# Preparation products of a chunked delta-rule attention: which engine makes them

## The chip, the cores and the metric

The kernel runs on one core of a Trainium2 chip. The metric is device time of one launch in microseconds. Three runs of the kernel before gave 1052.31 us as their median (1048.45 to 1052.65).

## The reference, cut to what matters

Attention is a recurrence over 768 steps for 32 heads of 40 by 40 state; its output feeds a mixture of experts with two of eight experts per token.

```python
for t in range(S):                       # attention, per head
    y[:, :, t] = einsum('bhd,bhde->bhe', rt, state)
    Sa = einsum('bhde,bhe->bhd', state, at)
    state = state * wt[:, :, None, :] - einsum('bhd,bhe->bhde', Sa, bt) \
            + einsum('bhd,bhe->bhde', vt, kt)
# experts: noisy top-2 gate, then for each expert e
h = maximum(x[mask] @ w1[e], 0.0)
out[mask] += top2_w[mask, k, None] * (h @ w2[e])
```

## The kernel before, in words

The recurrence is computed in chunks of 64 steps. There are twelve chunk positions for each of two halves `p` of the batch, so the main loop (`run`) has 24 turns `n`; turn `n` belongs to group `n//4` (six groups of two chunk positions), chunk `c` and half `p`. A group is prepared before its turns come, by three functions.

- `prepA(g,p)` loads the decays `raww` and the operands `rawba` (b and a). VectorE scans the decays (`Gx`, L495). ScalarE takes logarithm and exponential (L498, L499), VectorE makes a refined reciprocal `NH` from it (L501 to L504). Then come the products that this case is about: `NG_` (called G here), L506, a product of `Gx` with a scale; b by `NH`, L518; a by `NG_`, L520. `pack` splits each of b and a into two fp16 halves: the first by ScalarE (L459), the second by VectorE (L460); the result goes to DRAM (`d_ab`), and comes back in another layout (`st_ab`). `scoresL` multiplies b with a on TensorE, ScalarE copies the scores out (`lt`, `lo`, L556), and they go to DRAM (`scr`).
- `tsolve(g)` loads the scores of both halves as `X` (L563), masks them (L564) and inverts the triangular blocks in 30 pairs of a product and a sum (L570, L571). For groups zero and one this runs on VectorE, for groups two to five on GpSimd. The result goes to DRAM and comes back as `T` (L593).
- `prepC(g,p)` loads `rawk`, multiplies it by `NH` in two halves (L544), packs it (L459, L460) and stores it.

A turn (`chain`, `outp`, `pre`, `blocks`) is a chain of TensorE bursts (L470), ScalarE copies (`w` L473, `q` L652, `vu` L657, `sE` L630) and VectorE operations: `sfs` L625, `vu` L658, the state `Sst` L667, `ak` L606, `P` L680 twice, `uT` L474, `xT` L99, `xt` L691. L101 is the matmul of the expert gate, which ScalarE's `xT` (L98) feeds.

Buffers: one `rawba`, one `rawk`, one `Gx`, two `pk`, six `NG_` (`NGB`, so G of a group reuses the buffer of the group three before, after its last turn's transposes `pgm`), five `st_ab`. The preparation of group `g` is written into the loop seven turns (`LA`) and four turns (`LC`) ahead. A planner with its own cost estimates orders the instructions of every engine; the chain has a priority of 1500. Each engine then runs its list in that order. Before, G is made by GpSimd in all groups, b and a by VectorE in groups zero and one and by GpSimd after that, k by VectorE in group zero and by GpSimd after that. After attention the experts run, from 620 us on, almost wholly on TensorE.

Of the kernel before, what the change touches and what calls it, by code (L numbers as in the profile page):

```python
# [403 lines left out]
class Att:  # L404
# [81 lines left out]
    def prepA(s,p,g):  # L486
# [30 lines left out]
        dv=d.rearrange("l p x n->p l x n")  # L517
        (V if g in MD else nc.gpsimd).tensor_tensor(b_,b_,fl(NH),op=ALU.mult)  # L518
        s.pack(b_,-SC,1,1,V=V,out=lambda pk: nc.sync.dma_start(dv[:,:,1],pk))
        (V if g in MD else nc.gpsimd).tensor_tensor(a_,a_,fl(NG_),op=ALU.mult)  # L520
        s.pack(a_,-SC,0,1,V=V,out=lambda pk: nc.sync.dma_start(dv[:,:,0],pk))
# [244 lines left out]

BAB=1; RKB=1
SAB=5
MD=(0,1); MG=(); MK=(0,); TG=0
GA=-1; GC=-1  # L770
def HB(k=0): return [(h,b^k) for h in range(8) for b in range(2)]

# [125 lines left out]
```

## Time and profile before

| | value |
|---|---|
| median of the runs | 1052.31 us |
| profiled execution | 1041.7 us, span 1039.9 us |
| mean granted TensorE clock | 0.913 |
| busy: PE, DVE, ACT, POOL | 819.7, 543.8, 389.8, 399.2 us |
| hardware DMA queue q1 | 41.4% of the 16 engines' span |

DVE is VectorE, ACT is ScalarE, POOL is GpSimd, PE is TensorE. Busy time is an average over stages: attention with its preparation fills the first 620 us, the experts the rest. A profiled execution is one launch; its time differs from the runs' median.

### The profile page before, as it was taken

What the parts mean: (1) busy time and instruction counts of PE and PEld (TensorE: products, weight loads), DVE (VectorE), ACT (ScalarE), POOL (GpSimd) and SP (SyncE); (2) the same over time, 40 slices, a digit from 0 to 9 for tenths busy, and PEclk for the clock granted to TensorE, in tenths of its full rate; (3) what the DMA queues carried; (4) which work ended last, traced back from release to release, by engine and by line L of the source; (5) the groups of instructions that cost most, each with busy time, mean ns of one, the idle gap of its engine ahead of it and who ended that gap; (6) DMA issues with size and microseconds to landing.
All of it is one profiled execution on the core that took longest, in us unless ns stands there. A gap on an engine that the chain in (4) does not pass through costs nothing.

```text
span 1039.9 us, 27444 instructions
## 1 busy us (share of the span) xinstructions
PE 819.7 (79%) x11706; PEld 716.3 (69%) x11706; DVE 543.8 (52%) x1150; ACT 389.8 (37%) x820; POOL 399.2 (38%) x504
## 2 busy tenths in 40 slices
PE   0113456769888758888988789999999999999994
PEld 0113345557666646777766668899899999999994
DVE  9268568554469774338554753633443434343420
ACT  2202333335445433444442432525243535343420
POOL 6102241167659778219301004335151516160312
PEclk9999998779869866988996789999999999999998
DMA  4793996387588484473494402435252525252303
GB/s 119 177 235 91 254 249 152 93 226 198 124 213 249 126 206 110 110 160 108 138 280 147 135 14 43 120 93 133 58 133 67 131 64 133 61 137 59 35 8 37
DMA packets 127111, 135.88 MB, mean 131 GB/s; under 512 B 59249, under 2 KB 106805, under 8 KB 126901
## 3 DMA queue, kind: packets, MB, share of 16 engines
q1 hardware_dynamic: 116292, 114.90, 41.4%
q0 software_dynamic: 10688, 19.14, 9.7%
q8 instruction: 94, 1.54, 0.6%
q14 instruction: 37, 0.30, 0.1%
HBM read 96.25 MB, written 41.03 MB: 132 GB/s over the span
## 4 chain that ended last, share of the span: by engine, by line
PE 50%; POOL 13%; DMA 13%; DVE 11%; issue 5%; ACT 3%; SPq 2%; POOLq 0%; ACTq 0%; DVEq 0%
PE ph L287 17%; PE po L309 17%; POOL X L571 4%; POOL Tt L570 4%; DMA d_ab<-pk 3%; DMA rawk<-in_fm_dram 3%; PE psc L470 3%; PE pY L470 2%; PE pt L268 2%; PE pQ L470 2%; DVE X L571 1%; DVE Tt L570 1%; PE pW L470 1%; DMA d_k<-pk 1%; DMA X<-scr 1%
## 5 line engine op out<-in xcount | busy, mean ns | idle before, releaser
L311 POOL DMA_INDIRECT out_dram<-y,oi x56 | 92.2, 1647 | 233.7 <-ACT y L310 212.2
L290 DVE SCALAR_TENSOR_TENSOR hl<-ph,hh 128x256 fp32r<-128x256 f32 (+1 forms) x128 | 70.1, 555 | 120.4 <-ACT hh L288 113.2
L288 ACT ACTIVATE hh<-ph 128x320 fp32r<-128x320 f32 (+1 forms) x128 | 64.6, 518 | 147.7 <-PE ph L287 140.4
L470 PE MATMUL pQ<-w,T 32*32 32x40 f32 x2304 | 49.5, 229 | 48.4 <-ACT w L473 23.7
L470 PEld LDWEIGHTS pQ<-w,T 32*32 32x32 f32 x2304 | 42.2, 133 | 61.8 <-ACT w L473 26.3
L309 PE MATMUL po<-w2h,hh 128*128 128x320 f32 x384 | 74.8, 314 | 2.5 <-DVE y L304 1.9
L470 PE MATMUL psc<-RV,uT 128*64 128x128 f32 x384 | 65.3, 325 | 12.6 <-DVE P L680 12.1
L571 POOL TENSOR_TENSOR X<-X,Tt 128x30 f32<-128x30 f32 (+14 forms) x120 | 72.0, 600 | 8.2
L252 POOL DMA_INDIRECT xr<-xd,gi x56 | 53.7, 958 | 51.2 <-DVE oi L178 17.8
L309 PE MATMUL po<-w2h,hl 128*128 128x320 f32 x384 | 70.8, 311 | 0.0
L287 PE MATMUL ph<-xh,w1h 128*128 128x512 f32 (+1 forms) x256 | 69.7, 355 | 1.1 <-DVE hl L290 1.1
L570 POOL TENSOR_TENSOR Tt<-X 128x30 f32<-128x30 f32 (+14 forms) x120 | 67.2, 560 | 7.8
L287 PE MATMUL ph<-xh,w1l 128*128 128x512 f32 (+1 forms) x256 | 68.9, 350 | 0.0
L287 PE MATMUL ph<-xl,w1h 128*128 128x512 f32 (+1 forms) x256 | 68.6, 349 | 0.0
L470 PEld LDWEIGHTS psc<-RV,uT 128*64 128x64 f32 x384 | 51.7, 164 | 22.9 <-DVE P L680 13.0
L309 PE MATMUL po<-w2l,hh 128*128 128x320 f32 x384 | 65.7, 309 | 0.0
L309 PEld LDWEIGHTS po<-w2h,hh 128*128 128x128 f32 x384 | 61.0, 188 | 6.7 <-issue 2.3
L470 PE MATMUL psc<-RV 128*64 128x128 f32 x384 | 65.3, 325 | 0.0
L680 DVE TENSOR_TENSOR P<-psc,mk 128x512 f32<-128x512 f32 x48 | 32.9, 686 | 59.1 <-PE psc L470 59.1
L309 PEld LDWEIGHTS po<-w2h,hl 128*128 128x128 f32 x384 | 59.8, 188 | 0.5
L470 PEld LDWEIGHTS <-st_ab 120*64 120x64 f16 (+1 forms) x928 | 28.3, 123 | 44.1 <-issue 30.5
L309 PEld LDWEIGHTS po<-w2l,hh 128*128 128x128 f32 x384 | 58.6, 188 | 0.1
(314 smaller groups left out, 1936.2 us busy)
## 6 DMA issues: line engine op xcount, KB each, us to landing
w2r<-in_w_dram SPq DMA_DIRECT2D x8, 1280.0 KB
RV<-in_rv_dram SPq DMA_DIRECT2D x48, 192.0 KB
rawba<-in_fm_dram SPq DMA_DIRECT2D x24, 360.0 KB
d_ab<-pk SPq DMA_DIRECT2D x24, 360.0 KB
st_ab<-d_ab SPq DMA_DIRECT2D x36, 240.0 KB
w1r<-in_w_dram SPq DMA_DIRECT2D x8, 1024.0 KB
raww<-in_fm_dram SPq DMA_DIRECT2D x12, 365.6 KB
st_ab<-d_ab SPq DMA_DIRECT2D x24, 180.0 KB
```

What stands on the lines that cost most here:

```text
L252: k=t//128; nc.gpsimd.indirect_dma_start(out=X[:p,k if s.cap==CAP else 0],out_offset=None,in_=s.xd[int(w is not s.early[0])],in_offset=OFF ...
L268: for t,p in tiles(t0,n): nc.tensor.transpose(pt[:,t-t0:t-t0+p],x[:p,t//128,f0:f0+128],s.idm[:p,:p])
L287: for i,(a,b) in enumerate(mm): nc.tensor.matmul(ph[:,:n],a,b,start=i==0,stop=i==7)
L288: nc.scalar.activation(hh[:,f,:n],ph[:,:n],AF.Relu)
L290: if c.stop>c.start: nc.vector.scalar_tensor_tensor(o,ph[:,c],0.0,hh[:,f,c].bitcast(F32),op0=ALU.max,op1=ALU.subtract)
L309: s.lm=nc.tensor.matmul(po[:p],h[:,f,r],w[:,f],start=k==0,stop=k==23); k+=1
L311: st=nc.gpsimd.indirect_dma_start(out=s.out_d,out_offset=OFFS(ap=idx[:p,e,ii:ii+1],axis=0),in_=y[:p],in_offset=None,compute_op=ALU.add)
L470: def mm(s,*a,**k): return lambda: s.nc.tensor.matmul(*a,**k)
L570: eng.tensor_tensor(t,Xt[:,j:j+1,j+1:].to_broadcast([128,j,m]),Xt[:,0:j,j:j+1].to_broadcast([128,j,m]),op=ALU.mult)
L571: s.tl=eng.tensor_tensor(Xt[:,0:j,j+1:],Xt[:,0:j,j+1:],t,op=ALU.add)
L680: nc.vector.tensor_tensor(m,pp.rearrange("p i j t->p (i j) t"),s.mk.to_broadcast([128,8,64]),op=ALU.mult)
```

## The change

All three products go to VectorE in all groups. One other effect: the setup of the expert part's constants was ordered behind G of group zero (`after(pl)`); with 0 in `MG` it is not.

```diff
-MD=(0,1); MG=(); MK=(0,); TG=0
+MD=MG=MK=range(6); TG=0
```

The lines that read these names, unchanged (`V` is VectorE):

```python
s.pl=(V if g in MG else nc.gpsimd).tensor_tensor(NG_,Gx[:,:,0:64],nr[:,:,31:32]...,op=ALU.mult)  # L506
(V if g in MD else nc.gpsimd).tensor_tensor(b_,b_,fl(NH),op=ALU.mult)                             # L518
(V if g in MD else nc.gpsimd).tensor_tensor(a_,a_,fl(NG_),op=ALU.mult)                            # L520
(nc.vector if g in MK else nc.gpsimd).tensor_tensor(k1,k1,G['NH']...,op=ALU.mult)                 # L544, twice
with after(xd),(ExitStack() if 0 in MG else after(pl)): m.consts2(s.dm.bitcast(F32))              # run
```

## Rows read from the trace of the kernel before

**Rows 1.** Busy time by stretch: window, length, engines, granted clock, DMA share, GB/s.
```profile
85.00:160.00 75.00, 38.62 (x676) 32.11 (x678) 52.90 (x70) 28.29 (x54) 24.34 (x14) 1.00 0.84 218
160.00:410.00 250.00, 191.01 (x4405) 157.25 (x4403) 157.95 (x296) 103.00 (x238) 158.16 (x206) 0.80 0.66 170
```
**Rows 2.** Timeline of VectorE, state updates: start, length, engine, line, operation.
```profile
366.72 0.48 DVE L667 SCALAR_TENSOR_TENSOR Sst<-pS,gam 128x320 f32<-128x320 f32 x1
...
396.87 0.48 DVE L667 SCALAR_TENSOR_TENSOR Sst<-pS,gam 128x320 f32<-128x320 f32 x1
...
415.91 0.48 DVE L667 SCALAR_TENSOR_TENSOR Sst<-pS,gam 128x320 f32<-128x320 f32 x1
...
431.17 0.49 DVE L667 SCALAR_TENSOR_TENSOR Sst<-pS,gam 128x320 f32<-128x320 f32 x1 [1.63 <-PE pd L471]
```
**Rows 3.** Waits of ScalarE, 85 to 410 us: total, times, longest.
```profile
ACT pk L459 <- POOL rawba L518: 38.4, 8, 7.7
...
ACT pk L459 <- POOL rawba L520: 8.3, 6, 3.6
```
**Rows 4.** Timeline of ScalarE, packing; in brackets the idle time before and its end.
```profile
172.93 0.84 ACT L459 ACTIVATE pk<-rawba 120x768 f16<-120x768 f32 x1 [5.79 <-POOL rawba L518]
...
225.34 0.84 ACT L459 ACTIVATE pk<-rawba 120x768 f16<-120x768 f32 x1 [7.70 <-POOL rawba L518]
...
268.62 0.84 ACT L459 ACTIVATE pk<-rawba 120x768 f16<-120x768 f32 x1 [4.86 <-POOL rawba L518]
...
382.64 0.84 ACT L459 ACTIVATE pk<-rawba 120x768 f16<-120x768 f32 x1 [7.16 <-POOL rawba L518]
```
**Rows 5.** Timeline of TensorE: its idle time right behind those four.
```profile
174.15 1.27 PE L470 MATMUL pQ<-w,T 32*32 32x40 f32 x32 [6.31 <-ACT w L473]
...
228.49 0.25 PE L101 MATMUL pl<-wg,xT 128*128 128x16 f16 x3 [6.30 <-ACT xT L98]
...
269.92 0.76 PE L470 MATMUL pW<-q,lo 32*32 32x40 f32 x32 [1.76 <-ACT q L652]
...
384.77 1.28 PE L470 MATMUL pQ<-w,T 32*32 32x40 f32 x32 [6.72 <-ACT w L473]
```
**Rows 6.** Timeline of GpSimd: products of k ahead of the product of b.
```profile
168.89 2.09 POOL L544 TENSOR_TENSOR rawk<-rawk,NH 120x384 f32<-120x384 f32 x2 [18.81 <-DMA rawk<-in_fm_dram]
```
**Rows 7.** Timeline of VectorE, second half of the packing, with idle time before.
```profile
226.21 1.78 DVE L460 SCALAR_TENSOR_TENSOR pk<-rawba,pk 120x768 f16<-120x768 f32 x1 [7.47 <-ACT pk L459]
...
383.52 1.85 DVE L460 SCALAR_TENSOR_TENSOR pk<-rawba,pk 120x768 f16<-120x768 f32 x1 [7.46 <-ACT pk L459]
```
**Rows 8.** Groups by line: engine, count, busy us, mean ns, idle before.
```profile
L544 POOL TENSOR_TENSOR rawk<-rawk,NH 120x384 f32<-120x384 f32 x20 | 24.6, 1252 | 34.0 <-DMA rawk<-in_fm_dram 34.0
L518 POOL TENSOR_TENSOR rawba<-rawba,NH 120x768 f32<-120x768 f32 x8 | 14.6, 1825 | 6.5 <-DMA rawba<-in_fm_dram 6.5
...
L511 DVE TENSOR_TENSOR nge<-Gx,raww 120x12 f32<-120x12 f32 x10 | 6.4, 637 | 0.0
...
L544 DVE TENSOR_TENSOR rawk<-rawk,NH 120x384 f32<-120x384 f32 x4 | 2.0, 553 | 4.4 <-DMA rawk<-in_fm_dram 4.4
...
L514 DVE TENSOR_TENSOR gm<-nge,Gx 120x12 f32<-120x12 f32 x10 | 1.9, 191 | 0.0
L518 DVE TENSOR_TENSOR rawba<-rawba,NH 120x768 f32<-120x768 f32 x2 | 1.9, 952 | 1.0 <-DMA rawba<-in_fm_dram 1.0
```
**Rows 9.** Timelines of VectorE and GpSimd: a scan beside two steps of a solve.
```profile
333.16 2.08 DVE L495 TENSOR_TENSOR_SCAN Gx<-raww,d 120x780 f32<-120x780 f32 x1
...
332.94 0.66 POOL L570 TENSOR_TENSOR Tt<-X 128x234 f32<-128x234 f32 x1
333.68 2.00 POOL L571 TENSOR_TENSOR X<-X,Tt 128x234 f32<-128x234 f32 x1
```
**Rows 10.** Timeline of GpSimd: G products that waited, with what ended it.
```profile
279.48 1.48 POOL L506 TENSOR_TENSOR NG__4022<-Gx,raww 120x768 f32<-120x768 f32 x1 [6.07 <-PE pgm L471]
...
360.07 1.48 POOL L506 TENSOR_TENSOR NG__5505<-Gx,raww 120x768 f32<-120x768 f32 x1 [5.17 <-PE pgm L471]
```

## The prediction

> **What bounds the kernel now.** I read the busy times by stretch first. In the experts' stage, from 620 us on, TensorE is nearly always busy and nothing of the change runs there, so all of it must come from attention, and from the part where groups one to five are prepared, 85 to 410 us [rows 1]. There TensorE is busy 38.6 of 75 us and then 191.0 of 250 us, at a mean granted clock of 1.00 and 0.80; VectorE 52.9 + 158.0 = 210.9 of 325 us, 65%; GpSimd 182.5 us. No engine is full, so the turns are paced by waits. The next thing to read is the distance of two state updates: 30.2 us from 366.72 to 396.87, where group five is prepared, and 15.3 us from 415.91 to 431.17, where nothing is [rows 2]. A turn can thus go in half the time, and the preparation takes the rest.
>
> The view of waits says how. ScalarE waited 38.4 us, eight times, at L459 for the product of b (L518) from GpSimd, and 8.3 us, six times, for that of a (L520) [rows 3]. ScalarE runs its list in order: behind each packing stand the copies of the chain, and TensorE waits for those. The timelines show it: ScalarE idle 5.79, 7.70, 4.86 and 7.16 us [rows 4], and right behind each of the four TensorE idle 6.31, 6.30, 1.76 and 6.72 us, together 21.1 us, every time ended by a ScalarE copy [rows 5]. Why the product is late differs. Once the two products of k went first on GpSimd and themselves waited for their load [rows 6]; twice VectorE stood idle, 7.47 and 7.46 us, while GpSimd had the product to make [rows 7], and there part of the wait is that of the load of rawba, which the change leaves.
>
> **The change part by part.**
>
> *Products of b and a, groups two to five, 8 + 8.* One takes 1.825 us on GpSimd and 0.952 us on VectorE [rows 8]. The direct gain is 0.87 us each, and the product no longer stands behind solve steps and k products. What ScalarE's wait loses lies between 0.87 us and the whole wait. I take 4.4 of 6.31 us for the first of the four TensorE stalls (the k pair of 2.09 us and its load are out of the way), 2.1 of 6.30 for the second (the load is late, 0.87 plus a queue place), the whole 1.76 for the third, 2.6 of 6.72 for the fourth: 10.9 us. For the other waits of the 46.7 us, which are short or followed by little, 2 us. Sum -13 us; bounds 0 (the waits were all for loads) and -21 us (all four stalls go).
>
> *Products of k, groups one to five, 20 halves.* 1.252 us on GpSimd, 0.553 us on VectorE [rows 8]. They mostly wait for their load, 34.0 us of GpSimd's idle time, and are not late to ScalarE otherwise. Gain on the path: nothing; the wait that hides them is that for the load. If that cover went, 20 x 0.70 = 14 us would be to gain, which I leave out of the sum.
>
> *Products G, all groups, 12.* No row shows one on VectorE. I take 0.952 us, the row of L518, which has the same shape; the bounds are 0.553 us, the row of half that size, and 1.48 us, what GpSimd takes for it [rows 8, 10].
>
> *What VectorE gets.* 12 + 16 products at 0.952 us and 20 at 0.553 us: 26.7 + 11.1 = 37.7 us. It gets something back: the tiny L511 takes 637 ns where L514, of the same shape, takes 191 ns [rows 8]; L511 is issued right beside G. With G gone from GpSimd I take 10 x 0.45 = 4.5 us back. Net 33 us: VectorE's share of the 325 us goes from 65% to 75%. What of it lies on the path: a turn has nine VectorE operations that the chain waits for, and some 13 turns fall in the stretch, so 117 operations; each meets one of the new products with a chance of 33/325 = 0.10 and then waits for half of 0.95 us: 117 x 0.10 x 0.48 = 5.6 us. Bounds: 0 if the planner puts them into VectorE's idle 114 us, 33 us if all are in line with the chain. I take +5.6, near the lower bound, because VectorE stood idle at exactly the places where the products are needed [rows 7].
>
> *Solves of groups two to five.* They lose the products between their steps. Worth nothing by itself: no TensorE wait behind a solve's T shows among the four stalls, and a next solve waits for its X, not for GpSimd. What is late next is the load of rawba and the packing's DMA.
>
> *Setup of the expert constants, freed from its order.* GpSimd is idle then; nothing.
>
> The row of the scan shows that VectorE and GpSimd hinder each other: a solve step of 2.00 us beside a scan of 2.08 us, where the step before of the same shape took 0.66 us [rows 9]. The Trainium skill, "SBUF — State Buffer", section "Who interferes with whom", says that a VectorE instruction with two SBUF inputs and a GpSimd instruction that reads SBUF exclude each other for a whole instruction, whoever starts first; the trace agrees, with 2.00 against 0.66 us. This speaks against the change, since every moved product now runs beside the solves: by that rule each of the 30 products of groups three to five would wait half a step, 0.33 us, some 10 us on VectorE, of which the same sixth (5.6 of 33) reaches the chain: the sum would be 1.7 us worse, -5.7 us. I keep the sum without it, since the same rule gives back time where GpSimd's own products, twice as long, no longer hold VectorE.
>
> **Sum.** -13 + 5.6 = -7.4 us. The profiled execution took 1041.7 us, so 1034.3 us for one like it. That execution was 10.6 us below the median of the runs; the time is compared with runs, so 1052.3 - 7.4 = 1045 us.
>
> **The rivals.**
>
> *A. Products held on VectorE.* G reuses one of six buffers and may wait for a turn's transposes: 6.07 and 5.17 us on GpSimd, where only solves and products stood behind it [rows 10]. On VectorE the chain's P, vu and Sst stand behind it. If the planner places G too early by that wait in three of the six products of groups three to five, 3 x 5.6 = 17 us are added to every engine that waits for the chain: 1052.3 - 7.4 + 17 = 1062 us, slower. It decides from 7.4/5.6, two such places. For it: the planner's order is made from estimates. Against it: the scan that follows G on VectorE already waits for it and the order has kept that wait off the chain.
>
> *B. Loads, not products.* The ScalarE waits end with the load of rawba anyway, the gain is 0.87 us at each of the four stalls plus the 2 us for the rest, 5.5 us, and VectorE's 5.6 us take it back: 1052 us, no change. For it: VectorE's idle 7.46 us in front of the packing, in which the load was still on its way. Against it: two stalls of the four have another cause.
>
> *C. All stalls go, and the clock with them.* Four stalls 21.1 us, no cost on VectorE, and fewer idle gaps raise the granted clock of 0.80 in 160 to 410 us by 0.02 (each 0.01 is an estimated 2 us of TensorE's 191 us there): 21 + 4 = 25 us, 1027 us. For it: 15.3 us a turn is seen. Against it: VectorE's load is certain.
>
> *D. The planner reorders.* Another order of every engine for no reason of the products: some 10 us up, 1062 us.
>
> **How the numbers follow.** Forecast 0.45 (its own range 1035 to 1050), A 0.20, B 0.17, C 0.13, D 0.05. A difference below 0.5%, 5.3 us, can't be told from no change. Faster: C and 0.35 of the forecast's 0.45, 0.48. Same: B and the rest of the forecast, 0.27. Slower: A and D, 0.25. The range 1029 to 1063 us leaves out the ends of C and A.
>
> **What would show it right or wrong.** ScalarE's waits at L459 for a product should fall from 46.7 us to under 25 us, the waits for loads and packing's DMA stay; the four TensorE stalls should shrink to 10 us; VectorE's busy time should rise by 30 to 40 us and GpSimd's fall by some 72 us (24.6 + 14.6, the same 14.6 for a, and 12 x 1.48); the state updates of the turns around 366 us should come closer than 30.2 us. It is wrong if VectorE shows idle time in front of L506 ended by pgm, with P, vu or Sst behind it, or if the waits at L459 keep their length and only the engine's name in them changes.

## The result, and the profile after

The changed kernel takes 1036.85 us (median, 1035.52 to 1038.98), against 1051.84 us for the kernel before on the same chip: ratio 0.9883, 95% interval 0.9839 to 0.9926. It is faster: the medians differ by 15.0 us, the ratio is worth 12.3 us. The forecast was 1045 us with a range of 1029 to 1063. The time lies inside, but the gain is about twice the 7.4 us that were forecast, and it comes from elsewhere than the sum put it. The profiled execution took 1035.5 us, span 1033.7 us, mean granted clock 0.904.

The first view is the busy time by stretch of the kernel after, in the columns of [rows 1].

```profile
85.00:160.00 75.00, 43.14 (x801) 36.12 (x804) 54.98 (x89) 31.20 (x61) 0.00 (x0) 0.91 0.86 217
160.00:410.00 250.00, 185.97 (x4213) 154.04 (x4203) 165.32 (x319) 98.62 (x225) 110.76 (x177) 0.74 0.65 168
```

VectorE has 220.3 us of work in these 325 us, 68%, where [rows 1] have 210.9 us: 9.5 us more, though 46 of the 48 moved products fall into them, and the 48 add up to 42.1 us. GpSimd has nothing from 85 to 160 us. TensorE is idle 95.9 of the 325 us, where it was 95.4 before, and its granted clock is lower, 0.91 and 0.74 where it was 1.00 and 0.80. So in this part, from which the sum took its gain, TensorE has gained nothing.

The waits of ScalarE after, 85 to 410 us (total, times, longest), answer to [rows 3]:

```profile
ACT pk L459 <- DVE rawba L518: 22.7, 6, 7.2
...
ACT sfs L624 <- DVE Sst L667: 17.4, 8, 6.8
ACT pk L459 <- DVE rawba L520: 14.2, 5, 5.4
```

22.7 + 14.2 = 36.9 us, where the same two waits were 46.7 us. Mostly it is the engine's name that has changed. The same view for VectorE after (85 to 410 us) says why:

```profile
DVE rawk L544 <- DMA rawk<-in_fm_dram: 27.7, 8, 6.5
DVE P L680 <- PE psc L470: 16.8, 10, 5.1
DVE rawba L518 <- DMA rawba<-in_fm_dram: 14.5, 3, 5.5
```

The waits for the loads, 42.2 us, are now VectorE's own, and VectorE runs its list in order. Its timeline after shows what stands behind such a wait:

```profile
313.28 1.52 DVE L544 TENSOR_TENSOR rawk<-rawk,NH 120x384 f32<-120x384 f32 x2 [5.70 <-DMA rawk<-in_fm_dram]
314.72 0.55 DVE L99 SCALAR_TENSOR_TENSOR xT<-px,xT 128x384 f16<-128x384 f32 x1
315.19 0.47 DVE L667 SCALAR_TENSOR_TENSOR Sst<-pS,gam 128x320 f32<-128x320 f32 x1
```

The state update stands behind the product of k. ScalarE's next copy, in its own timeline, pays for it:

```profile
315.69 0.47 ACT L624 ACTIVATE sfs<-Sst 128x320 f16<-128x320 f32 x1 [6.00 <-DVE Sst L667]
```

TensorE's waits moved accordingly. Its view of waits, 85 to 410 us, first before, then after:

```profile
PE pQ L470 <- ACT w L473: 23.7, 9, 6.7
...
PE psc L470 <- DVE P L680: 9.9, 4, 5.1
```
```profile
PE psc L470 <- DVE P L680: 12.6, 4, 4.1
PE pY L470 <- DVE P L680: 9.1, 5, 4.1
PE pS L470 <- DVE vu L658: 8.2, 5, 4.1
PE pst L470 <- ACT sE L630: 6.8, 2, 6.5
...
PE pst L470 <- ACT sfs L624: 5.8, 3, 3.9
```

The wait for `w`, which stood behind the packing, is gone, and five for VectorE's results, or for copies behind these, stand in its place. So the two state updates that answer to [rows 2] are no closer, 30.8 us instead of 30.2 (VectorE's timeline after):

```profile
369.67 0.48 DVE L667 SCALAR_TENSOR_TENSOR Sst<-pS,gam 128x320 f32<-128x320 f32 x1
...
400.50 0.48 DVE L667 SCALAR_TENSOR_TENSOR Sst<-pS,gam 128x320 f32<-128x320 f32 x1
```

Where then is the gain? Each turn has one copy `q` (L652), so their start times cut attention into stretches, and the last `xt` (L691) ends it. In the profiled executions:

| us | before | after |
|---|---|---|
| start to the first `q` | 93.7 | 91.8 |
| first to 17th `q` (all moved products run up to here) | 364.7 | 365.0 |
| 17th to last `q` | 125.4 | 127.0 |
| last `q` to last `xt` (the tail) | 27.0 | 17.5 |
| last `xt`, the end of attention | 610.8 | 601.3 |
| last `xt` to the end of the span | 429.1 | 432.4 |

The last moved product starts at 403 us. Attention became 9.5 us shorter, and the stretches ahead of the tail give nothing of that together (-1.9, +0.3 and +1.6 us): it is the tail, in which no moved product runs. The tail holds the end of turn 22, the last but one, and turn 23. What differs there is the planner's order of the last two turns, and TensorE's clock. The busy times by stretch of before, then of after, for 580 to 590 and 590 to 600 us:

```profile
580.00:590.00 10.00, 7.02 (x187) 6.00 (x185) 6.06 (x28) 4.37 (x14) 0.65 (x3) 0.79 0.94 282
590.00:600.00 10.00, 7.22 (x75) 5.40 (x70) 6.11 (x21) 1.33 (x3) 0.00 (x0) 0.50 0.03 11
```
```profile
580.00:590.00 10.00, 9.54 (x232) 7.97 (x231) 8.65 (x40) 3.66 (x10) 0.40 (x2) 0.74 0.46 140
590.00:600.00 10.00, 6.85 (x116) 5.40 (x112) 3.63 (x7) 2.44 (x6) 0.00 (x0) 1.00 0.05 18
```

After, TensorE is busy 9.54 of 10 us, its level rises at 585 us and stays at 2.4 GHz; before, it is busy 7.02 of 10 us, and its level falls to 1.2 GHz at 589 us. TensorE's timeline has the same 32 matmuls, of turn 22, at both levels, before and after:

```profile
593.66 1.94 PE L470 MATMUL pY<-kb,P 128*64 128x40 f32 x32 [1.16 <-DVE P L680]
```
```profile
589.61 1.13 PE L470 MATMUL pY<-kb,P 128*64 128x40 f32 x32
```

Over the whole tail TensorE is busy 20.8 us before and 13.8 us after, with 279 and 275 matmuls on record, and idle 6.2 and 3.6 us. So some 7 of the 9.5 us are nearly the same matmuls that run shorter, and the rest are shorter waits. As the lower level itself lengthens busy time, busy shares alone don't tell whether the order brought the level or the other way round.

In VectorE's timeline the second P of turn 22 starts at 592.92 us before and at 588.87 us after, since the ranking of the last tokens (L133 and what follows it) comes between the two P before, and ahead of the first P after:

```profile
587.55 0.69 DVE L680 TENSOR_TENSOR P<-psc,mk 128x512 f32<-128x512 f32 x1 [0.38 <-PE psc L470]
...
590.63 0.17 DVE L133 TENSOR_TENSOR k<-pr,lim 128x16 f32<-128x16 f32 x1 [2.39 <-PE pr L127]
...
592.92 0.69 DVE L680 TENSOR_TENSOR P<-psc,mk 128x512 f32<-128x512 f32 x1
```
```profile
583.96 0.17 DVE L133 TENSOR_TENSOR k<-pr,lim 128x16 f32<-128x16 f32 x1 [0.45 <-PE pr L127]
...
586.46 0.68 DVE L680 TENSOR_TENSOR P<-psc,mk 128x512 f32<-128x512 f32 x1
...
588.87 0.68 DVE L680 TENSOR_TENSOR P<-psc,mk 128x512 f32<-128x512 f32 x1
```

One thing remains open. The profiled spans differ by 6.2 us, the medians by 15.0 us. The profiled execution of before lies 10 us below its median, that of after 1.3 us.

### The profile page after: what moved, and what is told of

It reads as the page before. It is cut to its first block, busy times and chain, and to the rows that moved or that the text cites. A ratio compares the mean times of both kernels' runs of the same rounds, so it can differ in the third digit from the quotient of the medians.

```text
span 1033.7 us, 27409 instructions
## 1 busy us (share of the span) xinstructions
PE 814.5 (79%) x11706; PEld 712.2 (69%) x11706; DVE 554.3 (54%) x1198; ACT 391.0 (38%) x820; POOL 321.1 (31%) x456
## 4 chain that ended last, share of the span: by engine, by line
PE 53%; DVE 21%; DMA 14%; issue 4%; ACT 4%; SPq 3%; POOL 0%; POOLq 0%; DVEq 0%; ACTq 0%
PE po L309 17%; PE ph L287 15%; DMA rawk<-in_fm_dram 6%; PE psc L470 4%; PE pY L470 3%; DMA d_ab<-pk 2%; PE pW L470 2%; PE pQ L470 2%; PE pt L268 2%; DVE X L571 2%; DVE Tt L570 2%; DVE w2l L244 1%; DVE pk L460 1%; PE pst L470 1%; DVE ohB L162 1%
## 5 line engine op out<-in xcount | busy, mean ns | idle before, releaser
L564 POOL TENSOR_TENSOR X<-X,tri 128x1024 f32<-128x1024 f32 x4 | 9.0, 2242 | 309.2 <-DVE ak L606 179.3
L470 PE MATMUL psc<-RV,uT 128*64 128x128 f32 x384 | 63.0, 317 | 17.0 <-DVE P L680 15.1
L571 POOL TENSOR_TENSOR X<-X,Tt 128x30 f32<-128x30 f32 (+14 forms) x120 | 72.2, 602 | 8.7
L570 POOL TENSOR_TENSOR Tt<-X 128x30 f32<-128x30 f32 (+14 forms) x120 | 70.1, 584 | 8.4
L470 PEld LDWEIGHTS psc<-RV,uT 128*64 128x64 f32 x384 | 50.0, 160 | 27.6 <-DVE P L680 16.5
L470 PE MATMUL pQ<-w,T 32*32 32x40 f32 x2304 | 46.7, 224 | 23.7 <-DMA T<-scr 23.1
L470 PEld LDWEIGHTS pQ<-w,T 32*32 32x32 f32 x2304 | 39.6, 128 | 36.3 <-issue 32.1
L470 PE MATMUL psc<-RV 128*64 128x128 f32 x384 | 63.1, 317 | 0.0
```

The source lines that it names most:

```text
L470: def mm(s,*a,**k): return lambda: s.nc.tensor.matmul(*a,**k)
L570: eng.tensor_tensor(t,Xt[:,j:j+1,j+1:].to_broadcast([128,j,m]),Xt[:,0:j,j:j+1].to_broadcast([128,j,m]),op=ALU.mult)
L571: s.tl=eng.tensor_tensor(Xt[:,0:j,j+1:],Xt[:,0:j,j+1:],t,op=ALU.add)
```

## The experiments

Ratios are to the kernel before in the same set (its medians: 1044.9, 1048.6, 1049.3 and 1044.2 us); they are not the quotients of the medians, from which they differ by up to 0.3%. All but the sixth and the last change only the line of constants, of which the new form is shown. The table collects what the rows of `q` and `xt` gave in one profiled execution of each, in us.

| kernel | ratio (95%) | first to 17th `q` | last `q` to last `xt` | last `xt` |
|---|---|---|---|---|
| before | 1 | 364.7 | 27.0 | 610.8 |
| after | 0.988 (0.984 to 0.993) | 365.0 | 17.5 | 601.3 |
| 1 early parts | 0.996 (0.993 to 0.999) | 360.9 | 27.8 | 607.4 |
| 2 late parts | 1.013 (1.008 to 1.018) | 379.0 | 17.5 | 619.1 |
| 3 a, b alone | 1.037 (1.033 to 1.041) | 404.0 | 28.3 | 652.1 |
| 4 G alone | 1.014 (1.011 to 1.018) | 382.6 | 28.4 | 631.6 |
| 5 whole again | 0.989 (0.983 to 0.994) | 361.9 | 17.4 | 601.2 |
| 6 setup ordered | 0.990 (0.987 to 0.994) | 362.3 | 17.6 | 603.9 |
| 7 whole without k | 1.015 (1.010 to 1.021) | 372.5 | 28.3 | 624.7 |
| 8 whole without early G | 1.002 (0.999 to 1.005) | 373.1 | 17.6 | 615.8 |
| 9 G of group 0 | 1.000 (0.996 to 1.003) | 366.7 | 17.6 | 608.5 |
| 10 k alone | 1.008 (1.004 to 1.011) | 362.3 | 27.9 | 616.2 |
| 11 early G, k of group 4 | 1.002 (0.999 to 1.006) | 377.4 | 17.5 | 620.5 |
| 12 last turns by hand | 1.001 (0.998 to 1.004) | 366.0 | 27.0 | 611.8 |

The first set took the change apart. Its theories were: T1, ScalarE's shorter waits at the packing in groups two to five; T2, the first stage, where G on GpSimd held VectorE's small products; T3, another order of the planner.

**1. The early parts alone** (groups zero and one).

```diff
-MD=(0,1); MG=(); MK=(0,); TG=0
+MD=(0,1); MG=(0,1); MK=(0,1); TG=0
```

> Only groups zero and one change: their G (four products) and group one's k (four halves) go to VectorE, groups two to five stay on GpSimd. Theory 1 (the gain is ScalarE's shorter waits at the packing of groups two to five): no change, 0 to -2 us, ratio 0.998 to 1.000. Theory 2 (the gain is the first stage, where a G on GpSimd held VectorE's own small products up, L511 1.46 us): most of the gain, -6 to -10 us, ratio about 0.992, first state update near 101.7 us instead of 109.0 us. Theory 3 (another order of all engines by the planner, no cause of the products): any value within 10 us either way.

Measured 1039.45 us, 0.996: some 4 us of the gain, between the two theories' numbers. The first state update came at 102.2 us, as T2 said, but the tail is long, so its gain is another than that of the whole change.

**2. The late parts alone** (groups two to five; the expectation of 8 calls them the title's part).

```diff
-MD=(0,1); MG=(); MK=(0,); TG=0
+MD=range(6); MG=(2,3,4,5); MK=(0,2,3,4,5); TG=0
```

> Only groups two to five change: their G, a, b and k go to VectorE; groups zero and one stay. Theory 1: nearly the whole gain, -8 to -14 us, ratio about 0.989. Theory 2: -2 to -5 us, and the state updates of the turns five to twelve no earlier than before. Theory 3: any value; with the first experiment it does not add up to the whole change's -15 us.

Measured 1055.84 us, 1.013, slower. T1, the first term of the sum, fell, and so did T2's number. The two parts together would give 1.009; the whole gives 0.988. They don't add up, as T3 said.

**3. The products of a and b alone.**

```diff
-MD=(0,1); MG=(); MK=(0,); TG=0
+MD=range(6); MG=(); MK=(0,); TG=0
```

> Only the products of b and a of groups two to five go to VectorE, G and k stay on GpSimd. Theory 1: most of the gain, -7 to -12 us. Theory 2: 0 to -3 us, since G still runs on GpSimd beside VectorE's chain of the preparation. Theory 3: any value within 10 us.

Measured 1080.44 us, 1.037, by far the slowest and outside of all three theories. Waits of VectorE in it, 85 to 460 us:

```profile
DVE rawba L518 <- DMA rawba<-in_fm_dram: 15.6, 3, 9.9
...
DVE rawba L520 <- POOL NG__5895 L506: 10.5, 1, 10.5
...
DVE rawba L520 <- POOL NG__4427 L506: 7.0, 1, 7.0
```

G, left on GpSimd, stands behind solve steps and the products of k there, and VectorE, which needs it for a, waits with the chain behind. It is like rival A in that a product holds up VectorE and the chain behind it, but what it waits for is GpSimd's list, not a buffer.

**4. G alone.**

```diff
-MD=(0,1); MG=(); MK=(0,); TG=0
+MD=(0,1); MG=range(6); MK=(0,); TG=0
```

> Only G goes to VectorE, in all groups; a, b and k of groups two to five stay on GpSimd. Theory 1: 0 to -3 us. Theory 2: -6 to -12 us, L511's mean near 0.2 us instead of 637 ns. A rival (G waits for its buffer in VectorE's list and holds the chain up): +5 us or more, with idle time in front of L506 ended by pgm.

Measured 1058.4 us, 1.014. ScalarE waited 40.0 us for GpSimd's product of b (85 to 460 us), so that wait is no shorter than before. L511's mean fell to 338 ns, but the gain that T2 saw in that didn't come. The rival had the size, but its sign, idle time in front of L506 ended by pgm, came to 1.9 us only. So the parts of 2, 3 and 4 are each slower alone, and the question for the next set was whether a whole chain on one engine (theory C) or the order of the planner (theory O) made the whole fast.

**5. The whole change again.** No edit against the changed kernel.

> The change once more, beside the three kernels of this set. Theory C (what counts is that the whole preparation of a half stays on one engine, so that no product is handed from GpSimd to VectorE and back): ratio to before 0.985 to 0.992, in the profile the first state update near 102 us and last xt near 601 us, as in the changed kernel's first profile. Theory O (the gain is an accident of the planner's order and differs little from no change): 0.995 or more.

Measured 1038.0 us, 0.989. First state update at 102.3 us, last `xt` at 601.2 us: the gain and its place come again, as theory C said.

**6. The whole change, the setup of the expert constants ordered as before.**

```diff
-with after(xd),(ExitStack() if 0 in MG else after(pl)): m.consts2(s.dm.bitcast(F32))
+with after(xd),after(pl): m.consts2(s.dm.bitcast(F32))
```

> The whole change, but the setup of the expert constants stays ordered behind G of group zero. Theory C: this setup runs on an idle GpSimd, so the ratio is that of the whole change, 0.985 to 0.992. Rival S (the freed setup gives part of what the first stage gained): the first state update comes at 105 us or later, ratio 0.994 or more.

Measured 1038.91 us, 0.990. The first state update came at 101.5 us, so rival S fell: the freed setup is worth nothing, as forecast.

**7. The whole change without k.**

```diff
-MD=(0,1); MG=(); MK=(0,); TG=0
+MD=MG=range(6); MK=(0,); TG=0
```

> G, a and b of all groups on VectorE, the products of k as before (GpSimd from group one on). Theory C: the chain Gx, G, a, b is whole on VectorE, and k mostly waits for its load, so nearly the whole gain stays: 0.987 to 0.993. Rival K (the gain comes from k: no late d_k of group one, and the end of attention, 27.0 us from the last q to the last xt before and 17.5 after, which so far was short only where k of the late groups was on VectorE): the last 27 us stay, ratio 0.997 to 1.005.

Measured 1063.43 us, 1.015. Theory C fell: the chain of a and b is whole on VectorE, and the kernel is slower than before. VectorE still waits for rawba, and TensorE for VectorE's P, the view of waits of each, 85 to 410 us:

```profile
DVE rawba L518 <- DMA rawba<-in_fm_dram: 26.0, 3, 10.3
```
```profile
PE psc L470 <- DVE P L680: 29.3, 5, 12.3
```

Its last 28.3 us are as long as before. The slowing went beyond what rival K expected, which had only the tail right.

**8. The whole change without G of groups zero and one.**

```diff
-MD=(0,1); MG=(); MK=(0,); TG=0
+MD=MK=range(6); MG=(2,3,4,5); TG=0
```

> The whole change, but G of groups zero and one stays on GpSimd (four products of 2.26 us beside VectorE's chain). Theory C: two groups are still split over two engines, the first state update comes at 109 us as before, and the ratio is above the whole change by some 7 to 10 us: 0.996 to 1.005. Rival K (the k of group one on GpSimd is what made the title's part alone slow, by ScalarE's 8.5 us wait for d_k at 132 us): 0.987 to 0.993.

Measured 1050.69 us, 1.002. Rival K fell. The early G is worth 1.3%, the range of theory C, but not for its reason: the first state update came at 103.7 us, not 109. What became longer is the time from the first to the 17th `q`, by 8 to 11 us against the whole, with G back on GpSimd in two groups only.

At this point all kernels fell into two classes, 17.4 to 17.6 us and 27.0 to 28.4 us from the last `q` to the last `xt`. From the last `q` but one to the last `xt`, the short class has one and the same order of VectorE's operations, the long class another (in 1, and later in 10, one `xt` stands a place later). The third set used that: the order of a kernel's list is known before it runs, so the class could be foretold (theory O; P stands for the products themselves).

**9. Only G of group zero moved**, two products, in a kernel with the short class of order.

```diff
-MD=(0,1); MG=(); MK=(0,); TG=0
+MD=(0,1); MG=(0,); MK=(0,); TG=0
```

> Only the two products G of group zero go to VectorE (and the setup of the expert constants is freed); everything else is as before. Theory O (half or more of the change's gain comes from the order in which the planner sets the last turns, in which no product runs any more, and any small change can flip that order): in this kernel VectorE's order of the last two turns is that of the changed kernel, so the last q to the last xt takes 17.5 us, not 27.0, and the ratio is 0.987 to 0.993. Theory P (the gain comes from the products on VectorE): two of 48 products are moved, 0.5 us each, so 0.998 to 1.002 and a tail of 27 us.

Measured 1047.08 us, 1.000. The tail is 17.6 us, as theory O said, and TensorE's clock in the last turn is the high one (its busy time by stretch, 600 to 610 us, columns as above):

```profile
600.00:610.00 10.00, 7.91 (x129) 6.47 (x128) 3.38 (x6) 2.42 (x6) 0.00 (x0) 1.00 0.06 21
```

The total is what theory P said: the turns ahead took 8.5 us more, first to last `q` 498.6 us where before has 490.1. Most of it, 6.5 us, lies between the 17th and the last `q`, where profiles of one and the same order differ too: 127.0, 129.4 and 132.4 us in after, 5 and 6. That the order changes far from the edit can be counted in the traces. Up to the 17th `q`, the moved products aside, at least 44 of VectorE's 504 operations and 24 of ScalarE's 367 stand elsewhere in 9 than before; between after, 5 and 6, and between before and 12, none does. So two moved products change the order of much that they don't touch, with some 8 us up here and 9 us down there.

**10. Only k moved, in all groups**, with the long class of order.

```diff
-MD=(0,1); MG=(); MK=(0,); TG=0
+MD=(0,1); MG=(); MK=range(6); TG=0
```

> Only the products of k go to VectorE, in all groups; G, a and b as before. In this kernel VectorE's order of the last turns is that of the kernel before. Theory O: the last q to the last xt takes 27 us as before, VectorE waits some 25 us for the loads of rawk with the chain behind it, and the ratio is 0.998 to 1.015. Theory P (k on VectorE is what the change gained by, since G, a and b alone took 1.015): 0.975 to 0.990.

Measured 1058.15 us, 1.008; tail 27.9 us; VectorE waited 32.5 us for rawk. Theory O held in all three, though its wait was to be some 25 us. Theory P fell: k, whose removal made the whole so slow in 7, gains nothing by itself.

**11. Early G and k of group four**, short class, chosen to beat the change.

```diff
-MD=(0,1); MG=(); MK=(0,); TG=0
+MD=MG=(0,1); MK=(0,4); TG=0
```

> G of groups zero and one and k of group four on VectorE, all else as before; VectorE's order of the last turns is that of the changed kernel. Theory O: the first groups are as in the kernel with only the early parts (ratio 0.996 there, last q to last xt 27.8 us), the tail is 17.5 us, so 0.984 to 0.990, no slower than the whole change. Theory P: G early and one group's k, 0.994 to 0.998.

Measured 1051.27 us, 1.002. The tail is 17.5 us as foretold, and the first turns lost it again: 377.4 us from the first to the 17th `q`, 16.5 us more than with the early parts of 1, from which it differs by two groups' k (groups one and four). Neither theory had the total.

**12. The kernel before, no product moved, the last turns' order set by hand.**

```diff
+# the ranking ahead of P of turn 22, on VectorE
+with (after(m.rl.ins) if n==22 else ExitStack()): nc.vector.tensor_tensor(m,pp.rearrange(...),...)   # L680
+# the ranking matmul ahead of the last turn's blocks, pu ahead of its first apply, on TensorE
+with (after(m.rm.ins) if n==22 else ExitStack()): s.blocks(O[n+1])
+with (s.tc.issue_after(s.pul.ins) if last and p else ExitStack()): s.warm(U,ND[0]); ...; s.apply(U,T,w1,range(4))
```

> The kernel before with no product moved. Only the order of the last two turns is set by hand, near to that of the changed kernel: TensorE's ranking matmul ahead of the blocks of the last turn, VectorE's ranking ahead of P of turn 22, the transposes of Ut ahead of the last apply. GpSimd and the loads keep their order, the other engines theirs up to turn 22. Theory O: up to the last q but one all is as before, the last q to the last xt falls from 27.0 to 17 to 20 us, and the ratio is 0.988 to 0.994, most of the change's gain without one of its products. Theory P (the short tail follows from the products, the order only goes along with them): the tail stays above 24 us, ratio 0.998 to 1.002.

Measured 1044.74 us, 1.001; tail 27.0 us. Theory O's numbers failed, and those of theory P came true. VectorE's timeline, and the busy times by stretch:

```profile
586.73 0.17 DVE L133 TENSOR_TENSOR k<-pr,lim 128x16 f32<-128x16 f32 x1 [0.69 <-PE pr L127]
...
590.77 0.69 DVE L680 TENSOR_TENSOR P<-psc,mk 128x512 f32<-128x512 f32 x1
```
```profile
580.00:590.00 10.00, 7.41 (x175) 6.06 (x175) 6.43 (x37) 4.89 (x16) 0.65 (x3) 0.67 0.89 286
590.00:600.00 10.00, 7.31 (x65) 5.89 (x65) 4.88 (x12) 1.23 (x3) 0.00 (x0) 0.50 0.06 19
```

The ranking came 3.9 us earlier, but my order held the first P to 590.77 us, 3.2 us later than before; TensorE was busy 7.41 of 10 us and its level fell as before. So the ranking's place alone is not it. Nor does theory P follow, as 9 has the short tail with two products of group zero moved, more than 500 us ahead of it. The hand-made order is not that of the changed kernel in every row, so whether the full order would bring the short tail with no product moved was not tried. As a near copy of before it also shows how well a profile repeats: the last `xt` at 611.8 and 610.8 us. Those of the whole change have it at 601.3, 601.2 and, in 6, 603.9 us.

## Why the prediction was right, and where it was not

The direction and the range were right, the place of the gain was not. Over the three profiles of the whole change (after, 5, 6) attention ends at 602.1 us on average, 8.7 us sooner: -1.7 us up to the first `q`, -1.6 to the 17th, +4.2 to the last, -9.5 in the tail. These three, with the same order, differ by 3.2 us from the first to the 17th `q` and by 5.4 us from there to the last, and of before there is one profile, so only the tail is clear of that spread. What the sum priced at -7.4 us, the work on the products, shows some -3.4 us, which can't be told from nothing. That the time fell inside the range is luck: it came from the tail, which has no term in the sum.

- *What bounds the kernel.* Right for the part that it reads, 85 to 410 us: waits pace the turns, not busy time. That all of the gain must come from this part was wrong.
- *Products of b and a, -13 us.* This step failed. It took ScalarE's wait for the product as lost once VectorE makes it. The wait fell by 9.8 us of 46.7 only, because it ended with the load more often than I allowed, and it was handed to an engine with more behind it: VectorE waits 42.2 us for loads with P, `vu` and the state behind. Before, GpSimd waited for these loads, 34.0 + 6.5 us [rows 8], with only solves and products behind it. Rival B had the cause (loads, not products) but not that the wait moves onto the chain. Of the signs, GpSimd's busy time fell by 78.1 us where 72 were forecast, but the waits at L459 stayed above 25 us, VectorE's busy time rose by 10.5 us in the whole execution and not by 30 to 40, and the state updates came no closer. Of the sign given for failure, the second half came true in the main: the waits lost a fifth, and the engine's name changed.
- *What VectorE gets, +5.6 us from 33 us of work.* Mis-sized, both parts. The work grew by 9.5 us, not 33, since with fewer products on GpSimd VectorE's own operations became faster. In the whole execution the moved products take 42.1 us on VectorE, somewhat over the 37.7 us of the sum, and its other 1150 instructions together 25.9 us less. L511 gave back 4.4 us, as the sum had it; that others would too had no term: L504 went from 1443 to 964 ns, the second half of the packing (L460, rawba) from 1294 to 1026 ns, one solve step of group one that stood beside products of k (L571, 128x220) from 1143 to 386 ns. What the moved products cost the chain showed as waits, not as work. The rows of L504, before and after, 85 to 410 us (count, busy us, mean ns, idle before):

```profile
L504 DVE TENSOR_TENSOR NH<-raww,Gx 120x768 f32<-120x768 f32 x8 | 11.5, 1443 | 0.1
```
```profile
L504 DVE TENSOR_TENSOR NH<-raww,Gx 120x768 f32<-120x768 f32 x8 | 7.7, 964 | 0.1
```

- The Trainium skill, "SBUF — State Buffer", section "Who interferes with whom", has a VectorE instruction with two SBUF inputs and a GpSimd instruction that reads SBUF exclude each other. These rows agree: of the eight L504 before, the three that began under a G product or a mask of GpSimd took 1.86, 2.17 and 2.76 us and the others 0.94 to 0.96 us; after, none took over 1.06 us. I used the rule for the cost that it adds beside the solves and under-rated what it gives back.
- *Products of k, nothing.* The reason was wrong: the load hides them on GpSimd, but on VectorE the wait for it, 27.7 us, stands ahead of the chain. By itself k costs 0.8% (10); without it the whole loses 2.7% (7 against 5). There is no price of k that holds in both. Beside solve steps a half took up to 1.00 us, where the sum had 0.553 us.
- *G at 0.952 us.* Right, 0.941 to 0.952 us, and up to 1.30 us beside a solve. Rival A did not come in the changed kernel, where no wait stands ahead of L506.
- *Rival C, all stalls go and the clock rises.* It did not come: the granted clock of 160 to 410 us fell from 0.80 to 0.74.
- *Setup of the constants, nothing.* Right (6).
- *Rival D, the planner reorders.* I gave it 0.05 and one sign. It weighs more than the products' own prices: 1, 8, 9 and 11 differ from their neighbours by a few products, and the time from the first to the 17th `q` goes from 360.9 to 377.4 us. How much of such a difference is the new order and how much the moved products themselves was not separated.

Shown: the place of the gain (three profiles), the two classes of tail, the clock that goes with each (14 profiles, 7 of each class), that the class was foretold three times from VectorE's order (9, 10, 11), and that the late parts alone lose. Argued only: that this order is the cause of the higher level and of the short tail. 12 set part of it by hand, and the tail stayed long, so the cause of the gain stays open.

## What to carry to other kernels

Before you move an operation to another engine, look at what it waits for: a wait for a load goes with it, and on the engine that serves the critical chain it can cost more than the faster instruction gives (k alone, 0.8% slower). In a kernel whose order a planner makes, the time of a small edit is that of a new order; cut the span at marks of the loop, see whether the gain lies where the edit does, and run one edit of no weight beside it (here two products moved 8 us in one stretch and 9 us back in another). Parts of such a change need not add up, so measure the whole, and don't credit the part of it that one had in mind.

## What the hardware showed unexpectedly

VectorE took on 42.1 us of products and was busy only 10.5 us longer in the whole execution (543.8 and 554.3 us), as its other operations took 25.9 us less with fewer products on GpSimd; instructions that overlap are the rest. And the same tail, with no moved work in it, took 17.5 or 27 us; from 590 to 600 us the granted clock was 1.00 (2.4 GHz) in the short one and 0.50 (1.2 GHz) in the long one, with TensorE busy 9.54 and 7.02 of 10 us in the stretch ahead.
